# A gated mix of a Fourier layer and a feed-forward layer: sums of the hidden layer formed by adding stores, and the second Strassen level for more products

## The chip, the cores and the metric

One core of one Trainium2 chip. The metric is the device time of one execution in microseconds (us), the median of several runs. Engines by the profile's names: PE (TensorE, matmuls), PEld (its weight loads), DVE (VectorE), ACT (ScalarE), POOL (GpSimd) and SP (SyncE); the last two only issue DMAs here, ACT next to none.

## The reference, cut to what matters

```
g   = sigmoid((x * gate_w).sum(-1))                        # x: 2048 x 1024
a   = x @ dft_hid_re.T ;  b = x @ dft_hid_im.T             # 1024 x 1024 each
y   = dft_seq_re @ a - dft_seq_im @ b                      # 2048 x 2048 each
h   = relu(x @ w1 + b1) ** 2                               # w1: 1024 x 3584
o   = h @ w2 + b2                                          # w2: 3584 x 1024
out = g * y + (1 - g) * o
```

All in float32. The Fourier matrices are inputs like others; nothing of their structure is used.

## The kernel before, in words

**Five stages, one after the other on TensorE:** x (a and b from x), c (y, and y * g), h part 0 (hidden columns 0 to 2047), h part 1 (2048 to 3583), o (the output). What one stage gives the next goes through HBM in blocks of 128 partitions x 2 x 512 floats, 512 KB (class Kept: `ab`, `h_far`, `gy`).

**Float32 from three matmuls.** An operand block is split into `hi`, its value rounded to fp32r by a ScalarE copy, and `lo`, the remainder, by a VectorE subtraction (class Operand, lines 315 to 327). Each product of 128 x 128 by 128 x 512 is three matmuls: hi hi, hi lo, lo hi (Group.run, line 393). So each operand costs one ACT and one DVE instruction, and each sum of blocks one more of DVE.

**Seven products for eight.** Each stage is one 2 x 2 block product by the Strassen-Winograd scheme: sums S1 to S4 of left blocks, T1 to T4 of right blocks, seven products (FACTORS, line 49), worked in the order 1, 2, 5, 6, 3, 7, 4 (WIDE, TALL_C, TALL_O). Product 5 is S1 x T1, 6 is S2 x T2, 7 is S3 x T3, 4 takes T4; 1 and 2 take plain blocks. The results are added up on their way from PSUM by DVE (`add`) or copied by ACT (`put`); an ACT copy into PSUM (`prepare`, line 380) seeds a group with an earlier result.

**The second level.** `twice` works a product by the same scheme once more, on its own quarters, at the price of more sums, halves and takings-up. In the x and h stages ("wide", 2 x 2 k-steps) a product has the second level or not (TWICE_X, TWICE_H): 7 steps of 4 x 6 = 24 matmuls in place of 8 (of 18 in part 1). In c and o ("tall", 8 and 7 k-steps) TWICE_C and TWICE_O tell for each product how many pairs of k-steps have it; a pair is 84 matmuls then and 96 without. With FIRST_C, FIRST_O a product's remaining k-steps are worked ahead of the pairs, as groups of their own.

**Where sums are made.** Mostly by DVE, in the slot of the loaded block. LAND_X, LAND_C, LAND_H and LAND_O name sums of which some (the number is that of the stage's k-steps and halves) are made by POOL instead: SP loads the one block and an accumulating DMA of POOL's queue adds the other in SBUF (Part.load, lines 259 to 264). T2 (FAR_TALL) is formed from T1 as stored to HBM ("copy") and loaded again. S1 to S4 of x, made in the x stage, are kept in HBM for the h stages (`shared`).

**What sets the order.** Nothing is issued as written: every operation is recorded (class Op), and `plan` (line 1039) sorts them, by a model of times, into one order for each engine, with 55 slots of 4 KB per partition as SBUF (SLOTS), handed out by due time, and four PSUM pairs. A block's slot is free once its last reader is done, a store's landing included. `emit` (line 1181) issues them in that order, and that is why nearly all of the profile stands on line 1194. Each DMA queue has at most eight DMAs under way (LANES). POOL carries all stores and the accumulating DMAs, SP the plain loads.

**The h stages and o.** A result block of h belongs to F-half i and token-half n; `target` (line 822) names where it goes in HBM, `final` (line 832) applies bias, relu and square on ACT and puts one store on the list. In o the right operands are blocks `h_far[j, q, 2 * n + c]`, so T1 = h(0, 1) + h(0, 0) and T3 = h(1, 1) + h(0, 1) by F-half and token-half; T1 is made by accumulating loads (LAND_O) and T3 by DVE, 14 blocks each.

Of the kernel before, what the change touches and what calls it, by code (L numbers as in the profile page):

```python
# [15 lines left out]
P = 128  # L16
# [1 line left out]
NF = F // P  # L18
SLOTS = 55
WIDE, TALL_C, TALL_O = ((1, 2, 5, 6, 3, 7, 4),) * 3  # L20
TWICE_X, TWICE_C, TWICE_O = (1, 2, 5, 3, 4), {1: 1, 2: 4, 3: 4, 4: 4, 5: 2}, {1: 2, 2: 3, 3: 3, 4: 3, 5: 1}
FIRST_C, FIRST_O = (2,), (2,)
WARM = 44
FAR_TALL, FAR_WIDE = ("T2",), ()
LAND_X, LAND_C, LAND_H, LAND_O = {"T1": 4, "T3": 2}, {"T1": 16, "T3": 8}, ({"T1": 4}, {"T1": 2, "T3": 2}), {"T1": 14}
SHARE = ("S1", "S2", "S3", "S4")
TWICE_H = (1, 2, 5, 3, 4), (1, 2, 5, 3, 4)

MM, MM_END, FIRST_MM = 0.2267, 0.18, 6.2
VEC, VEC_END, ACT, ACT_END = (0.086, 1.0417e-3), 0.39, (0.11, 0.84e-3), 0.41  # L30
# [23 lines left out]
def gated_mix_kernel(ctx: ExitStack, tc: tile.TileContext, x4, xn, w4, ct, w1a, w1b, w2, b1, b2, gw, out):  # L54
# [168 lines left out]
    class Kept:  # L223


        def __init__(self, name):
            self.at, self.done, self.left = fixed([P, 2, 512], name, pool=dram), False, 2
            self.at.count, self.at.box = 1024, (0, 2, 0, 512)

        def store(self, src, k, tiles):  # L230

            nc.gpsimd.dma_start(self.at[:, k:k + tiles, :], src[:, :tiles, :])
            self.left -= tiles
            self.done = not self.left

# [178 lines left out]
    class Sums:  # L414


        def __init__(self, get, sums, keep=False, far=(), lands=(), shared=None):

            self.get, self.sums, self.keep, self.far, self.made = get, sums, keep, far, {}
            self.lands, self.shared = lands, shared  # L420

        def of(self, key, width=512, near=False):
            if key in self.made:
                return self.made[key]
            if self.shared and key in self.shared:
                return self.shared[key]
            if key not in self.sums:
                if not self.keep:
                    return self.get(*key)
                b = self.get(*key)  # L430
                e = b if isinstance(b, (Near, View)) else Part(b, width=width)
            else:
                a, b, op = self.sums[key]
                e = Part(*(self.of(p, width).far() if p in self.far and not near else self.of(p, width) for p in (a, b)),
                         op, width, key in self.lands)
                if self.shared is not None and key in SHARE:
                    self.shared[key] = e.far()
            self.made[key] = e
            return e
# [57 lines left out]
                    ends[e] = len(steps)  # L497
        return ends

    def tall(left, right, ksteps, order, second, first, target, final, last=None, lands={}):  # L500

# [7 lines left out]
        right = {(q, c): Sums(lambda j, n, q=q, c=c: right_(j, n, q, c), SUMS_R, far=FAR_TALL, lands=spread(lands, 2 * q + c, 2 * ksteps)) for right_ in (right,)  # L509
                 for q in range(ksteps) for c in range(2)}  # L510
        keys = [(c, rp) for c in range(2) for rp in range(2)]
        c11, c12, c21, c22 = ({k: target(i, n, k) for k in keys} for i in range(2) for n in range(2))
# [285 lines left out]
    def x_stage():  # L798
        to = {}

        def target(i, n, k):
            near = Near("ab")
            to[near] = ab[n, 4 * i + 2 * k[0] + k[2], k[1]]
            return near

        def final(dst, ps, sign):
            if ps is not None:
                nc.scalar.activation(flat(dst.slot), flat(ps), AF.Copy, scale=float(sign))
            stores.append((to[dst], dst, 0, 2))

        wide(lambda i, j, m, q: x4[2 * i + m, j, q], lambda j, n, q, c: w4[n, c, j, q], 4, WIDE, TWICE_X, target,
             final, -1, True, lands=LAND_X, shared=shared)

    h_far = {(j, q, t): Kept(f"h{j}{q}{t}") for j in range(2) for q in range(7) for t in range(4)}

    def h_stage(part):
        rows = 3 if part else 4
        to = {}  # L820

        def target(i, n, k):
            m, c, rp = k
            near = Near("h")
            tile0 = 16 * part + 2 * rows * i + rows * m + 2 * rp
            if rows == 4:
# [71 lines left out]
    def c_stage():  # L898
        rows = [Row(n, False) for n in range(2)]
        to = {}  # L900

        def target(i, n, k):
            near = Near("y")
            to[near] = i, n, *k
            return near

        def final(dst, ps):
            i, n, c, rp = to[dst]
            nc.vector.tensor_tensor(dst.slot, dst.slot if ps is None else ps, rows[n].of(c).broadcast_to([P, 2, 512]),
                                    op=ALU.mult)  # L910
            rows[n].used()
            stores.append((gy[i, n, c, rp], dst, 0, 2))

        at = len(steps)
        tall(lambda i, j, q: ab[j, q, i], lambda j, n, q, c: ct[n, c, j, q], 8, TALL_C, TWICE_C, FIRST_C, target, final,
             lands=LAND_C)
        return at, rows


    def o_stage():  # L920
# [25 lines left out]
        def final(dst, ps):  # L946
# [3 lines left out]
            for k in range(2):  # L950
# [285 lines left out]
```

## Time and profile before

| | |
|---|---|
| median of 3 runs | 1858.7 us (1857.58 to 1859.08) |
| the profiled execution | 1859.77 us, span 1858.0 us |
| PE busy | 1841.6 us, 8126 matmuls (44 of them to warm up) |
| DVE busy | 1706.1 us, 1692 instructions |
| ACT busy | 1096.3 us, 1254 instructions |
| POOL busy | 143.3 us |
| DMA | 445.06 MB, mean 240 GB/s |
| granted TensorE clock | 0.998 of full speed |

The span runs from the first to the last instruction; the execution's own time is a little longer. Every row of a view is one line of the kernel, engine, operation and tile; since one line emits everything, a row is known by its tiles: `lo<-raw,hi` is the subtraction that makes lo from a loaded block, `sum<-raw` a sum of two loaded blocks, `raw<-raw` one made in place, `both` a half-wide hi and lo in one slot, `u`, `ab`, `y`, `h`, `o` results on their way. "x1938 | 755.1, 390 | 7.5 <-ACT hi" is the number, the busy time in us, the mean ns of one, the engine's idle time ahead of them, and what ended most of it. Stretches of the span (windows) give each engine's busy time and number of instructions in it, the granted clock and the share of time in which the 16 DMA engines were busy.

### The profile page before, as it was taken

The page shows a single profiled execution, that of the slowest core. Times are in us where ns is not written, and L with a number is a line of the kernel's source. Part 1 is how long each engine was busy: PE and PEld are TensorE (multiplying, and loading weights), DVE is VectorE, ACT ScalarE, POOL GpSimd, SP SyncE. Part 2 cuts the span into 40 slices and gives each one's busy share as a digit, 9 for nine tenths or more (in the row PEclk, how much of TensorE's full clock was granted, in tenths as well). Part 3 has the DMA queues.
Part 4 walks back from the last instruction along what each step waited for, and adds up shares of the span by engine and source line. Part 5 has one row for each costly group of instructions (what it writes and reads, how often), then busy time and mean ns, then how long its engine had stood idle before and what let it go on. Part 6 is the DMA issues. An engine that isn't in the chain of part 4 may idle for free.

```text
span 1858.0 us, 22135 instructions
## 1 busy us (share of the span) xinstructions
PE 1841.6 (99%) x8126; PEld 1521.0 (82%) x8126; DVE 1706.1 (92%) x1692; ACT 1096.3 (59%) x1254; POOL 143.3 (8%) x230
## 2 busy tenths in 40 slices
PE   8999999999999999999999999999999999999998
PEld 7888887888888888888888888888788888888887
DVE  8997999799899997899995999968999988999998
ACT  6474656354453553466684799767986544355452
POOL 0100200001110001000100001001100111000001
PEclk9999999999999999999999999999999999999999
DMA  7762989449998479534661857537693899839835
GB/s 238 262 236 93 379 304 400 158 154 288 301 376 324 144 264 364 211 126 167 162 242 61 301 181 228 183 104 227 238 337 108 251 305 378 335 132 360 332 127 200
DMA packets 128862, 445.06 MB, mean 240 GB/s; under 512 B 14176, under 2 KB 23664, under 8 KB 128752
## 3 DMA queue, kind: packets, MB, share of 16 engines
q1 hardware_dynamic: 96544, 329.97, 48.5%
q0 software_dynamic: 31920, 113.27, 19.5%
q8 instruction: 64, 1.05, 0.2%
q10 hardware_dynamic: 288, 0.39, 0.1%
q14 instruction: 46, 0.38, 0.1%
HBM read 356.53 MB, written 87.04 MB: 239 GB/s over the span
## 4 chain that ended last, share of the span: by engine, by line
PE 86%; ACT 5%; DVE 4%; issue 3%; DMA 1%; POOL 0%; SPq 0%; DVEq 0%; POOLq 0%; ACTq 0%
PE ps L1194 86%; ACT h L1194 2%; ACT hi L1194 2%; DVE lo L1194 1%; DVE h L1194 1%; DVE sum L1194 1%; DMA raw<-in_ct 0%; DMA h<-h 0%; DMA raw<-in_x 0%; ACT u L1194 0%; ACT ps L1194 0%; POOL h L1194 0%; DVE o L1194 0%; DVE u L1194 0%; DVE raw L1194 0%
## 5 line engine op out<-in xcount | busy, mean ns | idle before, releaser
L1194 PE MATMUL ps<-hi 128*128 128x512 f32 x1938 | 755.1, 390 | 7.5 <-ACT hi L1194 4.7
L1194 PE MATMUL ps<-hi,lo 128*128 128x512 f32 x1938 | 753.7, 389 | 0.6 <-DVE lo L1194 0.6
L1194 PE MATMUL ps<-lo,hi 128*128 128x512 f32 x1938 | 753.9, 389 | 0.4 <-DVE lo L1194 0.4
L1194 ACT ACTIVATE hi<-raw 128x1024 fp32r<-128x1024 f32 (+2 forms) x375 | 380.4, 1034 | 250.2 <-DVE raw L1194 125.1
L1194 DVE TENSOR_TENSOR lo<-raw,hi 128x1024 fp32r<-128x1024 f32 (+2 forms) x375 | 441.1, 1194 | 44.1 <-ACT hi L1194 27.6
L1194 PE MATMUL ps<-hi,both 128*128 128x512 f32 x1512 | 467.0, 389 | 0.0
L1194 PEld LDWEIGHTS ps<-hi 128*128 128x128 f32 x1938 | 364.2, 188 | 86.7 <-ACT hi L1194 4.3
L1194 PEld LDWEIGHTS ps<-hi,lo 128*128 128x128 f32 x1938 | 364.0, 188 | 77.0 <-DVE lo L1194 1.0
L1194 PEld LDWEIGHTS ps<-lo,hi 128*128 128x128 f32 x1938 | 364.0, 188 | 76.3 <-DVE lo L1194 1.3
L1194 ACT ACTIVATE hi<-sum 128x1024 fp32r<-128x1024 f32 x228 | 233.3, 1035 | 190.8 <-DVE sum L1194 155.6
L1194 PEld LDWEIGHTS ps<-hi,both 128*128 128x128 f32 x1512 | 283.8, 188 | 59.3 <-ACT ps L1194 0.4
L1194 PE MATMUL ps<-lo,both 128*128 128x512 f32 x756 | 294.1, 389 | 0.0
L1194 DVE TENSOR_TENSOR lo<-sum,hi 128x1024 fp32r<-128x1024 f32 (+1 forms) x228 | 269.0, 1196 | 18.5 <-PE ps L1194 10.2
L1194 DVE TENSOR_TENSOR raw<-raw 128x1024 f32<-128x1024 f32 (+1 forms) x192 | 227.8, 1203 | 13.1 <-DMA raw<-h 3.6
L1194 DVE TENSOR_TENSOR sum<-raw 128x1024 f32<-128x1024 f32 (+2 forms) x168 | 171.8, 1031 | 6.0 <-PE ps L1194 3.0
L1194 ACT ACTIVATE u<-ps 128x1024 f32<-128x1024 f32 x110 | 106.4, 971 | 101.3 <-PE ps L1194 81.1
L1194 PEld LDWEIGHTS ps<-lo,both 128*128 128x128 f32 x756 | 141.9, 188 | 29.5
L1194 DVE TENSOR_TENSOR sum<-raw,sum 128x1024 f32<-128x1024 f32 (+2 forms) x126 | 137.8, 1095 | 4.7 <-PE ps L1194 3.6
L1194 DVE TENSOR_TENSOR h<-h,ps 128x1024 f32<-128x1024 f32 (+1 forms) x92 | 98.2, 1082 | 20.1 <-ACT u L1194 18.4
L1194 ACT ACTIVATE both<-sum 128x512 fp32r<-128x512 f32 x108 | 66.2, 624 | 54.6 <-DVE sum L1194 39.4
L1194 ACT ACTIVATE ps<-u 128x1024 f32<-128x1024 f32 x82 | 80.1, 978 | 24.7 <-DVE u L1194 6.9
L1194 ACT ACTIVATE h<-h,b1c 128x512 f32<-128x512 f32 x112 | 75.8, 709 | 4.3 <-DVE h L1194 4.1
(56 smaller groups left out, 814.3 us busy)
## 6 DMA issues: line engine op xcount, KB each, us to landing
raw<-in_ct SPq DMA_DIRECT2D x129, 512.0 KB, 7.9
raw<-h SPq DMA_DIRECT2D x120, 512.0 KB, 7.3
raw<-in_w SPq DMA_DIRECT2D x92, 512.0 KB, 8.3
raw<-ab SPq DMA_DIRECT2D x72, 512.0 KB, 9.3
raw<-copy SPq DMA_DIRECT2D x62, 512.0 KB, 4.9
raw<-in_x SPq DMA_DIRECT2D x59, 512.0 KB, 6.0
h<-h POOLq DMA_DIRECT2D x48, 512.0 KB, 4.4
copy<-raw POOLq DMA_DIRECT2D x46, 512.0 KB, 6.9
```

The source lines that it names most:

```text
L1194: made = getattr(real[op.engine], op.name)(*(actual(a) for a in op.args), **{k: actual(v) for k, v in op.kwargs.items()})
```

## The change

It makes T1 and T3 of h in HBM while h is written. For each k-step and half there is one more kept block for T1 and one for T3 (`sums_far`). A finished block of h is stored to each sum in which it has a part: the first store to a sum is plain, the second an accumulating one (Kept.store). The token-halves of o change places (`1 - n` in o's `target` and in its right operands), so that now T1 = h(0, 0) + h(0, 1) and T3 = h(0, 0) + h(1, 0) by F-half and token-half; h(0, 0), the first part of both, stands nowhere else and is no longer stored by itself. In o these sums are loaded as they are; T1 (NEAR_O) is loaded once into a slot and used from there.

The second level is given to product 6 of h part 0 (TWICE_H), to one more pair of k-steps of o's product 5 and to one pair of its product 6 (TWICE_O); product 2 of o no longer works its remaining k-step first (FIRST_O). POOL makes four T3 sums fewer in c, T1 and T3 four times each and not twice each in h part 1, and none in o (LAND_C, LAND_H, LAND_O).

```
-TWICE_X, TWICE_C, TWICE_O = (1, 2, 5, 3, 4), {1: 1, 2: 4, 3: 4, 4: 4, 5: 2}, {1: 2, 2: 3, 3: 3, 4: 3, 5: 1}
-FIRST_C, FIRST_O = (2,), (2,)
+TWICE_X, TWICE_C, TWICE_O = (1, 2, 5, 3, 4), {1: 1, 2: 4, 3: 4, 4: 4, 5: 2}, {1: 2, 2: 3, 3: 3, 4: 3, 5: 2, 6: 1}
+FIRST_C, FIRST_O = (2,), ()
...
-LAND_X, LAND_C, LAND_H, LAND_O = {"T1": 4, "T3": 2}, {"T1": 16, "T3": 8}, ({"T1": 4}, {"T1": 2, "T3": 2}), {"T1": 14}
+LAND_X, LAND_C, LAND_H, LAND_O = {"T1": 4, "T3": 2}, {"T1": 16, "T3": 4}, ({"T1": 4}, {"T1": 4, "T3": 4}), {}
 SHARE = ("S1", "S2", "S3", "S4")
-TWICE_H = (1, 2, 5, 3, 4), (1, 2, 5, 3, 4)
+NEAR_O = ("T1",)
+TWICE_H = (1, 2, 5, 3, 4, 6), (1, 2, 5, 3, 4)
...
     class Kept:
-        def __init__(self, name):
-            self.at, self.done, self.left = fixed([P, 2, 512], name, pool=dram), False, 2
+        def __init__(self, name, more=0):
+            self.at, self.done, self.left, self.more = fixed([P, 2, 512], name, pool=dram), False, 2 + more, more
...
         def store(self, src, k, tiles):
-            nc.gpsimd.dma_start(self.at[:, k:k + tiles, :], src[:, :tiles, :])
+            if self.left <= self.more:
+                nc.gpsimd.dma_start(self.at[:, k:k + tiles, :], src[:, :tiles, :], accum_op=ADD)
+            else:
+                nc.gpsimd.dma_start(self.at[:, k:k + tiles, :], src[:, :tiles, :])
...
     class Sums:
...
             if self.shared and key in self.shared:
-                return self.shared[key]
+                if key not in self.near:
+                    return self.shared[key]
+                self.made[key] = Part(self.shared[key])
+                return self.made[key]
...
-    h_far = {(j, q, t): Kept(f"h{j}{q}{t}") for j in range(2) for q in range(7) for t in range(4)}
+    h_far = {(j, q, t): Kept(f"h{j}{q}{t}") for j in range(2) for q in range(7) for t in range(4) if j + t // 2}
+    sums_far = {(q, c): {k: Kept(f"{k}{q}{c}", 2) for k in ("T1", "T3")} for q in range(7) for c in range(2)}
...
-            if rows == 4:
-                to[near] = h_far[i, 2 * m + rp, 2 * n + c], 0, 2, tile0
-            else:
-                to[near] = (h_far[i, 6, 2 * n + c], m, 1, tile0) if rp else (h_far[i, 4 + m, 2 * n + c], 0, 2, tile0)
+            q, at, tiles = (2 * m + rp, 0, 2) if rows == 4 else (6, m, 1) if rp else (4 + m, 0, 2)
+            far = [h_far[i, q, 2 * n + c]] if i + n else []
+            far += [sums_far[q, c][k] for k in (("T1", "T3"), ("T1",), ("T3",), ())[2 * i + n]]
+            to[near] = far, at, tiles, tile0
...
-            stores.append((kept, dst, at, tiles))
+            for k in kept:
+                stores.append((k, dst, at, tiles))
+            dst.uses = len(kept)
...
         def target(i, n, k):
             near = Near("o")
+            n = 1 - n
...
-        tall(lambda i, j, q: w2[i, j, q], lambda j, n, q, c: h_far[j, q, 2 * n + c], 7, TALL_O, TWICE_O, FIRST_O, target,
-             final, last, LAND_O)
+        tall(lambda i, j, q: w2[i, j, q], lambda j, n, q, c: h_far[j, q, 2 * (1 - n) + c], 7, TALL_O, TWICE_O, FIRST_O,
+             target, final, last, LAND_O, sums_far)
...
                 dst.store(src.slot, k, tiles)
-                src.used() if isinstance(src, Part) else src.drop()
+                src.used()
```

`tall` hands `shared` on to the sums of its right operands, and the other stages set `dst.uses = 1` for their single store.

More of the change, by code (lines that the diff above doesn't have):

```diff
@@ L414, in gated_mix_kernel, with __init__ @@
     class Sums:
-        def __init__(self, get, sums, keep=False, far=(), lands=(), shared=None):
+        def __init__(self, get, sums, keep=False, far=(), lands=(), shared=None, near=()):
+            self.near = near
             self.get, self.sums, self.keep, self.far, self.made = get, sums, keep, far, {}
@@ L498, in seven, with tall @@
         return ends
-    def tall(left, right, ksteps, order, second, first, target, final, last=None, lands={}):
+    def tall(left, right, ksteps, order, second, first, target, final, last=None, lands={}, shared=None):
         left = {q: Sums(lambda i, j, q=q: left_(i, j, q), SUMS_L, far=FAR_TALL) for left_ in (left,) for q in range(ksteps)}
-        right = {(q, c): Sums(lambda j, n, q=q, c=c: right_(j, n, q, c), SUMS_R, far=FAR_TALL, lands=spread(lands, 2 * q + c, 2 * ksteps)) for right_ in (right,)
+        right = {(q, c): Sums(lambda j, n, q=q, c=c: right_(j, n, q, c), SUMS_R, far=FAR_TALL, lands=spread(lands, 2 * q + c, 2 * ksteps),
+                               shared=shared and shared[q, c], near=NEAR_O) for right_ in (right,)
                  for q in range(ksteps) for c in range(2)}
@@ L809, in final @@
             stores.append((to[dst], dst, 0, 2))
+            dst.uses = 1
         wide(lambda i, j, m, q: x4[2 * i + m, j, q], lambda j, n, q, c: w4[n, c, j, q], 4, WIDE, TWICE_X, target,
              final, -1, True, lands=LAND_X, shared=shared)
-    h_far = {(j, q, t): Kept(f"h{j}{q}{t}") for j in range(2) for q in range(7) for t in range(4)}
+    h_far = {(j, q, t): Kept(f"h{j}{q}{t}") for j in range(2) for q in range(7) for t in range(4) if j + t // 2}
+    sums_far = {(q, c): {k: Kept(f"{k}{q}{c}", 2) for k in ("T1", "T3")} for q in range(7) for c in range(2)}
     def h_stage(part):
@@ L912, in final @@
             stores.append((gy[i, n, c, rp], dst, 0, 2))
+            dst.uses = 1
         at = len(steps)
```

## Prediction

> **What bounds the kernel now.** I read the page first, then its chain, then stretches of the span cut where one Strassen product ends and the next begins.
>
> ```profile
> span 1858.0 us, 22135 instructions
> PE 1841.6 (99%) x8126; PEld 1521.0 (82%) x8126; DVE 1706.1 (92%) x1692; ACT 1096.3 (59%) x1254; POOL 143.3 (8%) x230
> ...
> PE 86%; ACT 5%; DVE 4%; issue 3%; DMA 1%; POOL 0%; SPq 0%; DVEq 0%; POOLq 0%; ACTq 0%
> ...
> L1194 PE MATMUL ps<-hi 128*128 128x512 f32 x1938 | 755.1, 390 | 7.5 <-ACT hi L1194 4.7
> L1194 PE MATMUL ps<-hi,lo 128*128 128x512 f32 x1938 | 753.7, 389 | 0.6 <-DVE lo L1194 0.6
> L1194 PE MATMUL ps<-lo,hi 128*128 128x512 f32 x1938 | 753.9, 389 | 0.4 <-DVE lo L1194 0.4
> ...
> L1194 PEld LDWEIGHTS ps<-hi 128*128 128x128 f32 x1938 | 364.2, 188 | 86.7 <-ACT hi L1194 4.3
> ```
>
> The reader is to see that TensorE is busy all the time, and holds 86% of the chain; VectorE at 92% is close behind. Busy says nothing of pace: a row's 390 ns is the length of one pipelined matmul. The pace comes from a stretch without a stall, below: 520.0 us for 2295 matmuls is 0.2266 us each. The program has 8126 less 44 warm-up matmuls = 8082; at that pace they fill 1831.4 us. The other 26.6 us of the span are start, tail and stalls.
>
> ```profile
> core 0: us, PE busy (x) PEld busy (x) DVE busy (x) ACT busy (x) POOL busy (x), PEclk, DMA share, GB/s
> 49.20:125.30 76.10, 76.10 (x337) 63.02 (x336) 75.38 (x67) 42.85 (x44) 9.30 (x16) 1.00 0.71 242
> 320.00:840.00 520.00, 520.00 (x2295) 430.57 (x2295) 475.89 (x485) 256.36 (x297) 33.88 (x48) 1.00 0.71 247
> 695.40:782.50 87.10, 87.10 (x386) 72.12 (x385) 69.42 (x67) 37.07 (x41) 5.98 (x8) 1.00 0.84 298
> ...
> 896.70:972.90 76.20, 76.20 (x338) 63.10 (x337) 75.43 (x67) 58.48 (x65) 8.01 (x14) 1.00 0.63 209
> 972.90:1016.40 43.50, 43.50 (x194) 36.02 (x193) 22.82 (x20) 20.89 (x21) 0.70 (x2) 1.00 0.24 82
> 1016.40:1054.50 38.10, 38.10 (x170) 31.55 (x169) 37.40 (x34) 25.50 (x30) 2.14 (x4) 1.00 0.64 226
> 1054.50:1098.00 43.50, 43.50 (x194) 36.02 (x193) 39.17 (x35) 43.15 (x51) 4.27 (x8) 1.00 0.54 200
> 1098.00:1136.80 38.80, 38.67 (x170) 31.37 (x169) 38.80 (x37) 34.80 (x44) 4.82 (x9) 1.00 0.72 260
> 1136.80:1224.90 88.10, 86.55 (x379) 70.72 (x378) 84.45 (x88) 71.20 (x91) 8.24 (x13) 1.00 0.64 208
> ...
> 1319.10:1350.30 31.20, 29.16 (x128) 23.51 (x127) 30.61 (x34) 30.20 (x43) 4.87 (x10) 1.00 0.90 317
> 1350.30:1489.30 139.00, 138.99 (x613) 114.81 (x612) 133.25 (x146) 94.95 (x116) 9.30 (x13) 1.00 0.70 233
> 1489.30:1638.90 149.60, 149.60 (x661) 123.92 (x660) 132.65 (x125) 64.88 (x67) 16.60 (x25) 1.00 0.90 324
> 1638.90:1706.90 68.00, 68.00 (x301) 56.32 (x300) 67.11 (x72) 37.48 (x44) 0.00 (x0) 1.00 0.64 237
> 1706.90:1851.20 144.30, 144.30 (x637) 119.22 (x635) 141.56 (x147) 66.11 (x75) 7.19 (x10) 1.00 0.63 237
> ```
>
> Stalls can be read off: a stretch's length less its own matmuls (a row also counts the one or two across its edges) at 0.2266. 1098.0 to 1136.8 is product 4 of h part 0, 168 matmuls: 0.7 us lost. 1136.8 to 1224.9 is products 1, 2, 5 of part 1, 378 matmuls: 2.4 lost. 1319.1 to 1350.3 is product 4 of part 1, 126 matmuls: 2.6 lost. In all three DVE is busy almost without a break (38.80 of 38.80, 84.45 of 88.10, 30.61 of 31.20). So the bound is TensorE's count of matmuls, and where that bound is broken VectorE breaks it.
>
> **The Trainium skill** says otherwise on the first point. Its page "Perfetto Trace Analysis", section "Identifying the Most-Contended Engine", holds matmul occupancy to be no measure of the distance from the limit and puts the busy share of the weight loads in its place. By that, PEld at 82% would leave 18%, and a removed matmul would be worth a weight load at most: 48 of them, at the 188 ns of the LDWEIGHTS row, 9.0 us. Here the row of 320 to 840 differs: PEld is 83% where TensorE never waits, so 83% is the ceiling for this form, and I stay with the pace.
>
> **The change, part by part.** Counts are from the two programs' instruction lists.
>
> *Matmuls.* Product 6 of h part 0 takes the second level: 7 steps of 24 in place of 8, 24 fewer. In the output stage product 5 takes it for one more pair of k-steps and product 6 for a first pair; a pair is 84 matmuls in place of 96, so 24 fewer. Together 48, to 8034: 48 x 0.2266 = **10.9 us less**. Unsplitting product 2 (FIRST_O) changes no count.
>
> *VectorE.* The prices:
>
> ```profile
> L1194 DVE TENSOR_TENSOR lo<-raw,hi 128x1024 fp32r<-128x1024 f32 x347 | 417.2, 1219 | 37.6 <-ACT hi L1194 22.0 <-ACT u L1194 5.5 <-PE ps L1194 5.3
> L1194 DVE TENSOR_TENSOR both<-sum,both 128x512 fp32r<-128x512 f32 x108 | 72.9, 685 | 1.2 <-ACT both L1194 1.2
> L1194 DVE TENSOR_TENSOR raw<-raw 128x768 f32<-128x768 f32 x12 | 11.4, 953 | 2.7 <-DMA raw<-in_w1b 2.7
> ```
> ```profile
> 1103.04 1.22 DVE L1194 TENSOR_TENSOR h<-ps,u 128x1024 f32<-128x1024 f32 x1
> 1104.17 1.22 DVE L1194 TENSOR_TENSOR lo<-sum,hi 128x1024 fp32r<-128x1024 f32 x1
> 1105.30 1.22 DVE L1194 TENSOR_TENSOR h<-ps,u 128x1024 f32<-128x1024 f32 x1
> ```
>
> Back to back, one of 1024 starts 1.13 to 1.14 us after the one before, so 0.085 of its 1.22 overlaps; I take 1.135, and the same 0.085 off the others: 0.60 for 512, 0.87 for 768. Then:
> - h part 0, product 6: 6 more lo parts, 8 second-level sums, 14 more takings-up from PSUM (the adds onto c12 stay): 28 x 1.135 = +31.8 us.
> - Output stage: sums T1, T3 now arrive summed, so the 14 T3 adds go (T1's 14 were made by DMA already). Two more second-level pairs bring 2 lo, 14 half-wide lo, 8 sums, 8 half-wide sums, 8 takings-up: 4 x 1.135 + 22 x 0.60 = +17.8.
> - c stage: four T3 sums fewer are landed by DMA: +4.5. h part 1: four more are: -3.5.
>
> In all +50.6 us on an engine with 152 us idle. ScalarE's number of instructions does not change (1252); at 59% I cost it at nothing, covered by the matmuls.
>
> Whether it fits is a matter of place. I added up, for each stretch of matmuls, the VectorE work in its list up to the last instruction that these matmuls wait for, at the prices above (us; TensorE's time at 0.2266):
>
> | products | TensorE | VectorE due before | after |
> |---|---|---|---|
> | h part 0: 1, 2, 5 | 114.2 | 115.9 | 119.3 |
> | 6 | 43.5, after 38.1 | 20.4 | 37.5 |
> | 3 | 38.1 | 38.6 | 37.5 |
> | 7, 4 and h part 1: 1, 2, 5 | 167.2 | 162.4 | 167.0 |
> | h part 1: 6, 3 | 61.1 | 42.6 | 46.0 |
> | 7, 4 | 61.1 | 60.2 | 57.5 |
> | output: 1, 2 | 138.7 | 122.1 | 135.0 |
> | 5, 6 | 149.5, after 144.1 | 138.2 | 125.8 |
> | 3 | 68.0 | 59.3 | 80.0 |
> | 7, 4 | 144.1 | 135.2 | 135.0 |
>
> Product 6 of part 0 was VectorE's rest (22.82 of 43.50 busy); it now comes to 37.5 in 38.1. The trace shows that such products run without loss: 49.2 to 125.3 and 896.7 to 972.9 are pairs of them (75.4 of 76.1 and 75.43 of 76.20 busy, TensorE full). The 3.4 us more that are due in products 1, 2, 5, and as much in each of the two products ahead, can come from the rest in product 7 of c (69.42 of 87.10 busy). Then 167.0 us are due in 167.2 where 162.4 lost 3.1 (0.7 + 2.4) before: from nothing to the whole 4.6 more; I take +2, near the middle, as the margin falls from 4.8 to 0.2. Part 1's products 7, 4 have 2.7 less due: from -2.6 (that whole stall) to 0; I take -1. In the output stage product 3 is owed 12.0 more than its time, and products 5, 6 ahead of it have 18.3 spare: 0 if VectorE runs 12 us ahead, as c's product 7 shows it can (17.7 idle ahead of products with more due than their time), to 12.0 if it can't; I take +1, near the first. Stalls: **+2 us**.
>
> *Stores and loads.* 34 more DMAs on POOL's queue (260 for 226), 14 fewer on SP's (628 for 642). h's 64 stores become 48 (the h of F-half 0, token-half 0 is no longer kept by itself), and 64 stores of sums come, half of them adding. No store that adds into HBM is in the trace; nearest are the plain store and the adding load.
>
> ```profile
> q0 software_dynamic: 31920, 113.27, 19.5%
> ...
> h<-h POOLq DMA_DIRECT2D x48, 512.0 KB, 4.4
> ...
> raw<-h POOLq DMA_DIRECT2D x14, 512.0 KB, 10.0
> ```
> ```profile
> L1194 POOL DMA_DIRECT2D h<-h x64: 534/534/731, 921.8 to 1372.4; - x64
> ...
> L1194 POOL DMA_DIRECT2D raw<-h x14: 851/858/915, 1452.0 to 1525.4; - x14
> ```
>
> So one lies between 4.4 and 10.0 us to landing and between 0.53 and 0.86 us of POOL; I take 10 and 0.86, the row that adds. POOL's time is hidden behind an engine at 8%. The DMA engines have room: 0.24 to 0.72 busy over h part 0; 24 more stores of 512 KB there are 12.6 MB. POOL's queue (q0) moved 113.27 MB in 19.5% of 1858 us, 313 GB/s; so 40 us in 273, or 67 if the 16 that add move twice their bytes: 0.15 to 0.25 of share more. Each adding store waits on the store that it adds to; in POOL's list that stands at least 15 places earlier, and POOL lets only eight be under way, so this wait is over by the time POOL gets there. What is queued behind a waiting store are other stores, and the slot of h that both read comes free only with the second. That makes slots late, not matmuls, unless the free ones run out: 0 here, the rival below prices it. SP's queue gets shorter, and the output stage, its fullest (0.90 from 1489 to 1639), loses the 14 adding loads of T1 and 14 loads: from 0 to a little below.
>
> **Sum:** span 1858.0 - 10.9 + 2 = 1849.1. The profiled execution took 1859.77, 1.8 more than its span and 1.1 above the median of 1858.7; against the median, 1858.7 - 8.9 = **1849.8, so 1850**.
>
> **The rivals.**
> 1. *VectorE becomes the bound.* Against it: every row of the table but output 3 fits. For it: two rows have margins of 0.2 and 0.6 us in place of 4.8 and more, and no lost time is made up. Both upper ends paid, 4.6 + 12.0 = 16.6, gives 1858.7 - 10.9 + 16.6 = 1864; half of it 1856. I call it 1853.5 to 1862.
> 2. *The adding stores hold the slots: slower.* Place: the four bursts of h in which a finished half goes out (ends of products 3 and 4 in either part), eight tiles of two stores each, eight under way at a time. If a store lands at 10.0 in place of 4.4, the second round holds its slot 5.6 us longer, loads or operands have no slot, and TensorE waits: 4 x 5.6 = 22, 1858.7 - 8.9 + 22 = 1872. It decides for slower at 3.2 us a burst (8.9 + 3.7 over four). For it: the chain of before already runs through such a store, in the stretch that lost 2.6:
>
> ```profile
> 1328.94 7.46 DMA h<-h
> ```
>
> Against: 55 slots, and of those 2.6 us VectorE alone can be the cause. The Trainium skill ("DMA: Bandwidth & Descriptors", "Rules for kernel authors") says that an accumulate reads its destination and writes it later, with nothing holding the bytes between, so that it has to wait for the earlier DMA's semaphore. By that rule this wait is real; no run here shows it for HBM yet.
> 3. *Stalls shrink:* product 4 of part 1 loses nothing, nor does the output stage: 1858.7 - 10.9 - 2.6 = 1845.
> That the change doesn't do what it says is out: the lists show 48 matmuls fewer and the 32 adding stores.
>
> **How the numbers follow.** Forecast, 1846 to 1853.5: 0.62. Rival 1: 0.20. Rival 2: 0.08. Rival 3, 1846 and below: 0.10. A measurement of this kernel can tell about 0.2%, 3.7 us, from no change. Faster than 1855.0: 0.62, 0.10 and 0.08 of rival 1 make 0.80; within, the rest of rival 1: 0.12; slower: 0.08. The range: 1845 to 1857.5, which leaves out rival 2, the top of rival 1 and a little of rival 3.
>
> **What would show it.** Right: 8078 matmuls, 0.2266 apart outside the stalls; product 6 of part 0 near 38 us with VectorE full; VectorE's busy time near 1750; stalls beside start and tail near 10 us. Wrong: TensorE waiting on lo or sum over output product 3 (rival 1), on POOL's stores or landings near the ends of the h parts (rival 2); adding stores landing much later than 10 us.

## The result, and the profile after

The changed kernel takes **1852.6 us** (median; 1851.9 to 1854.4), the one before 1858.7 beside it: a ratio of 0.9969, 95% interval 0.9958 to 0.998. The forecast was 1850.0 in a range of 1845.0 to 1857.5. The profiled execution took 1852.40 us with a span of 1850.6; the one of before 1859.77 and 1858.0. Between the two spans lie 7.4 us, between the two medians 6.1.

The page of the kernel after: busy time and chain, then the two large DMA queues, then the stores (512 KB each, median us to landing).

```profile
span 1850.6 us, 22073 instructions
PE 1831.6 (99%) x8078; PEld 1511.9 (82%) x8078; DVE 1753.4 (95%) x1746; ACT 1090.8 (59%) x1254; POOL 169.2 (9%) x264
...
q1 hardware_dynamic: 94016, 323.15, 48.0%
q0 software_dynamic: 37072, 127.43, 22.5%
...
PE 82%; DVE 7%; ACT 4%; issue 3%; DMA 3%; POOL 0%; SPq 0%; DVEq 0%; ACTq 0%; POOLq 0%
...
T<-h POOLq DMA_DIRECT2D x48, 512.0 KB, 10.0
```

The 48 matmuls are gone (8126 to 8078), VectorE has its 47 us more (1706.1 to 1753.4), and TensorE's part of the chain falls from 86 to 82%, for VectorE 7 (4), DMA 3 (1). Where that sits is seen in stretches cut at the products' ends, as in the prediction: h part 0 products 6, 7, 4; part 1 products 1, 2, 5 together, and 4; output products 5 and 6 together, and 3.

```profile
973.30:1011.40 38.10, 38.10 (x170) 31.52 (x169) 37.77 (x35) 11.39 (x12) 0.00 (x0) 1.00 0.38 125
1049.40:1093.00 43.60, 43.60 (x194) 36.08 (x193) 39.97 (x35) 41.18 (x49) 10.81 (x16) 1.00 1.04 331
1093.00:1134.30 41.30, 38.57 (x169) 31.34 (x168) 40.80 (x38) 37.45 (x48) 8.44 (x13) 1.00 0.74 247
1134.30:1221.90 87.60, 86.63 (x380) 70.76 (x380) 87.21 (x90) 73.13 (x94) 19.30 (x29) 1.00 0.95 299
1316.00:1346.50 30.50, 29.13 (x127) 23.50 (x126) 30.34 (x34) 28.54 (x41) 9.54 (x15) 1.00 0.96 313
1485.50:1629.70 144.20, 144.20 (x638) 119.38 (x637) 143.44 (x145) 77.15 (x86) 10.46 (x18) 1.00 0.73 259
1629.70:1699.10 69.40, 68.30 (x301) 56.22 (x300) 68.57 (x74) 43.91 (x51) 0.00 (x0) 1.00 0.61 214
```

In the order of the columns: length; busy time and number on PE, PEld, DVE, ACT, POOL; clock; DMA share; GB/s. A stretch's own matmuls at 0.2265 us, taken from its length before rounding, leave what it lost (us; the prediction took 0.2266, which moves none of the first four differences):

| stretch | before | after | difference | forecast |
|---|---|---|---|---|
| h part 0, product 4 | 0.75 | 3.33 | +2.6 | +2 for this row and the next |
| h part 1, products 1, 2, 5 | 2.54 | 1.89 | -0.6 | (in the row above) |
| h part 1, product 4 | 2.65 | 1.97 | -0.7 | -1 |
| output product 3 | 0.05 | 1.49 | +1.4 | +1 |
| start of the x stage, tail | 11.43 | 12.28 | +0.8 | 0 |
| all else | 3.56 | 3.54 | 0.0 | 0 |

48 x 0.2265 = 10.9 less and 3.5 more lost make the 7.4 of the spans. The sizes are near the forecast; what doesn't fit is that product 4 of part 0, which the forecast held no worse than its neighbours, now loses as much by itself as the first two rows together did before. Here are the longest wait of TensorE between 1030 and 1350 us (total, times, longest), then the chain of the same place, in order of time (start, length, what), and then ScalarE's wait for one of the loads issued from 1045 to 1092 us.

```profile
PE ps L1209 <- DVE h L1209: 2.3, 1, 2.3
```
```profile
1029.87 36.05 PE ps L1209 x159
...
1065.94 16.02 DMA raw<-in_x
...
1081.99 1.06 ACT hi L1209
1083.06 1.23 ACT h L1209 x2
```
```profile
  ACT hi L1209: 2.1, 1
```

TensorE waits for VectorE; but the chain goes on back, from VectorE (nearly without a break from 1094 to 1140 us) to ScalarE and from there to one load of x that took 16.0 us to land, in the stretch whose DMA share is 1.04 (it was 0.54; the share of a stretch can come out a little over 1). Of before, that stretch's row in the prediction also tells what the forecast didn't read from it: ScalarE was busy 43.15 of 43.50 us there already.

**The theories.** *DMA:* the adding stores fill the DMA engines over product 7 of part 0, a load is late, and behind it everything is. *VectorE:* it has more due than there is time for, as the forecast had it, and the late load only happens to be there. A third came up on the way: *ScalarE* has no rest in that product and hands the lateness on.

### The profile page after: what moved, and what is told of

Read it like the earlier page. It is cut to its first block, busy times and chain, and to the rows that moved or that the text cites. A ratio compares the mean times of both kernels' runs of the same rounds, so it can differ in the third digit from the quotient of the medians.

```text
span 1850.6 us, 22073 instructions
## 1 busy us (share of the span) xinstructions
PE 1831.6 (99%) x8078; PEld 1511.9 (82%) x8078; DVE 1753.4 (95%) x1746; ACT 1090.8 (59%) x1254; POOL 169.2 (9%) x264
## 3 DMA queue, kind: packets, MB, share of 16 engines
q0 software_dynamic: 37072, 127.43, 22.5%
## 4 chain that ended last, share of the span: by engine, by line
PE 82%; DVE 7%; ACT 4%; issue 3%; DMA 3%; POOL 0%; SPq 0%; DVEq 0%; ACTq 0%; POOLq 0%
PE ps L1209 82%; DVE lo L1209 3%; ACT h L1209 2%; DMA raw<-in_x 2%; ACT hi L1209 2%; DVE h L1209 1%; DVE o L1209 1%; DVE sum L1209 1%; DMA raw<-in_ct 0%; DMA h<-h 0%; DVE u L1209 0%; DVE both L1209 0%; ACT ps L1209 0%; DVE raw L1209 0%; POOL h L1209 0%
## 5 line engine op out<-in xcount | busy, mean ns | idle before, releaser
L1209 PE MATMUL ps<-hi 128*128 128x512 f32 x1866 | 727.0, 390 | 8.6 <-ACT hi L1209 3.5
L1209 PE MATMUL ps<-hi,lo 128*128 128x512 f32 x1866 | 725.9, 389 | 0.6 <-DVE lo L1209 0.6
L1209 PE MATMUL ps<-lo,hi 128*128 128x512 f32 x1866 | 725.7, 389 | 0.4 <-DVE lo L1209 0.4
L1209 PE MATMUL ps<-hi,both 128*128 128x512 f32 x1624 | 501.9, 389 | 1.1 <-DVE both L1209 1.1
L1209 ACT ACTIVATE hi<-sum 128x1024 fp32r<-128x1024 f32 x244 | 249.7, 1036 | 198.3 <-DVE sum L1209 140.2
L1209 PEld LDWEIGHTS ps<-hi,both 128*128 128x128 f32 x1624 | 304.7, 188 | 65.2 <-DVE both L1209 1.9
L1209 PE MATMUL ps<-lo,both 128*128 128x512 f32 x812 | 315.9, 389 | 0.0
L1209 DVE TENSOR_TENSOR lo<-sum,hi 128x1024 fp32r<-128x1024 f32 (+1 forms) x244 | 288.2, 1196 | 12.3 <-PE ps L1209 8.8
L1209 DVE TENSOR_TENSOR raw<-raw 128x1024 f32<-128x1024 f32 (+1 forms) x178 | 211.1, 1205 | 5.6 <-DMA raw<-in_x 1.8
L1209 DVE TENSOR_TENSOR sum<-raw,sum 128x1024 f32<-128x1024 f32 (+2 forms) x135 | 147.5, 1094 | 3.7 <-PE ps L1209 2.8
L1209 ACT ACTIVATE both<-raw 128x512 fp32r<-128x512 f32 x87 | 53.8, 624 | 46.3 <-DVE raw L1209 21.2
```

Source lines behind the costliest of these rows:

```text
L1209: made = getattr(real[op.engine], op.name)(*(actual(a) for a in op.args), **{k: actual(v) for k, v in op.kwargs.items()})
```

## The experiments

**1. All adding stores issued as plain ones, in the same order.**

```
+        keep = {k: v for k, v in op.kwargs.items()
+                if k != "accum_op" or getattr(op.args[0].base, "name", "")[:1] != "T"}
```

> The changed kernel, every instruction in the same place, but the 32 adding stores of T1 and T3 are issued as plain stores (the second overwrites the first, so T1 and T3 hold one term only). Theory A, VectorE: product 4 of h part 0 loses 3.3 us because VectorE has more due than it has time; then nothing changes there, 3.3 us lost, time 1852.6. Theory B, DMA: the adding stores fill the DMA engines from 1040 to 1090 us, a load of x lands after 16 us and the operands behind it are late; then the loss falls to about 0.8 us as before the change, and the time is near 1850. Output product 3 loses 1.5 us by both.

1849.9 us, 0.9953 (0.9937 to 0.997). Every T1 and T3 of h holds one of its two terms alone. Product 4 of part 0 lost 1.10; part 1's products 1, 2, 5 lost 1.9 and output product 3 lost 1.48, both as in the changed kernel. The two stretches of products 7 and 4 of part 0, and the queue of POOL's DMAs, in this run:

```profile
1049.30:1092.80 43.50, 43.50 (x194) 36.03 (x193) 41.45 (x37) 43.19 (x51) 8.52 (x16) 1.00 0.83 337
1092.80:1131.90 39.10, 38.31 (x169) 31.45 (x168) 39.06 (x37) 35.25 (x46) 6.92 (x13) 1.00 0.71 259
```
```profile
q0 software_dynamic: 36560, 127.43, 20.4%
```

The same bytes on POOL's queue take 20.4% of 1848.3 us in place of 22.5% of 1850.6: 377 and 416 us of all 16 engines. So adding costs 39 us over 14.7 MB (24 stores of 512 KB, 8 of 256), about 1.4 us for each 512 KB, where 512 KB of this queue cost 1.6 on the mean (377 us for 127.43 MB, its accumulating loads included). An adding store is about two plain ones. VectorE has the same work, and the 2.2 us at product 4 are gone: the theory DMA holds there. Output product 3 loses the same with and without adding.

**2. VectorE relieved, in the same order.** Eight in-place adds of h and four of o work on half their columns.

```
+HALF = {("h", "ps"): range(28, 36), ("o", "u"): range(1, 4), ("o", "ps"): range(5, 6)}
...
+            if seen[kind] in HALF.get(kind, ()):
+                args = [a[:, 0:1, :] if len(a.shape) == 3 else a[:, 0:512] for a in args]
```

> The changed kernel, every instruction in the same place, but twelve in-place adds of VectorE work on half of their columns (the other half keeps the earlier value): eight of h between 1082 and 1125 us, 8 x 0.53 = 4.3 us less work, and four of o between 1646 and 1656 us, 2.1 us less. Theory A, VectorE: product 4 of h part 0 loses at most 1 us in place of 3.3, and output product 3 nothing in place of 1.5: 1849. Theory B, DMA: product 4 of part 0 still loses 2 to 3.3 us, output product 3 nothing: 1851.

1850.4 us, 0.9958 (0.9943 to 0.9972). The halves left out are missing from h and o. Product 4 of part 0 lost 0.14 although the load still took 15.4 us; but part 1's product 1 lost 2.48 in place of 0.99, and output product 3 lost 0.40. So both are right for product 4: the load comes late, and VectorE has nothing to make it up with. Part of the gain is lost again 40 us on, behind a second late load (11.1 us of the chain). That load is as late in the changed kernel (11.4 us from issue to landing, 6.0 in the kernel before); there, behind the loss at product 4, products 1 and 2 of part 1 lost only 1.3. Output product 3 follows VectorE's work.

**3. Without the second level of product 6 of part 0**, planned anew.

```
-TWICE_H = (1, 2, 5, 3, 4, 6), (1, 2, 5, 3, 4)
+TWICE_H = (1, 2, 5, 3, 4), (1, 2, 5, 3, 4)
```

> The changed kernel without the second level for product 6 of h part 0, planned anew: 24 matmuls more, 5.4 us. Theory A, VectorE: with its rest in product 6 back, product 4 of part 0 loses 0.8 us as before the change: 1852.6 + 5.4 - 2.5 = 1855.5. Theory B, DMA: the stores are still there, product 4 still loses about 3 us: 1858.

1862.9 us, 1.0025 (1.0014 to 1.0036): slower than before the change. Both numbers missed. The profiled execution was the slowest of the seven, 1866.8 us, so the losses that follow are above those of the median. VectorE has its rest in product 6 back (24.4 us idle), and yet product 4 of part 0 lost 5.0 us and part 1's product 1 lost 6.8. The two long DMAs of this run's chain between 1000 and 1200 us, its waits of TensorE from 1000 to 1360, and three stretches:

```profile
1055.03 23.16 DMA raw<-in_w1a
1143.52 17.20 DMA raw<-in_x
```
```profile
PE ps L1209 <- DVE u L1209: 3.9, 1, 3.9
PE ps L1209 <- DVE h L1209: 3.7, 3, 2.9
```
```profile
1130.00:1134.00 4.00, 1.10 (x5) 0.56 (x4) 4.00 (x5) 4.00 (x6) 1.12 (x3) 1.00 1.02 159
1134.00:1142.00 8.00, 7.96 (x28) 6.43 (x29) 7.12 (x7) 7.94 (x12) 5.81 (x9) 0.79 1.06 318
1164.00:1176.00 12.00, 8.12 (x25) 6.22 (x24) 11.41 (x12) 7.41 (x10) 5.95 (x6) 0.72 1.09 322
```

Loads land after 17 and 23 us, TensorE stands for 2.9 and 3.9 us, and behind each stall the granted clock is half for a while ((1 - 0.79) x 8 x 2 = 3.4 us and, from 0.72 over 12 us, 6.7). With less for VectorE to do it got worse, so VectorE's work alone doesn't set the loss. Since the plan is another one, the run doesn't part the stores from the place that the plan gives the loads.

**4. The output stage's second level as before**, the sums still made by adding stores; planned anew.

```
-TWICE_X, TWICE_C, TWICE_O = (1, 2, 5, 3, 4), {1: 1, 2: 4, 3: 4, 4: 4, 5: 2}, {1: 2, 2: 3, 3: 3, 4: 3, 5: 2, 6: 1}
-FIRST_C, FIRST_O = (2,), ()
+TWICE_X, TWICE_C, TWICE_O = (1, 2, 5, 3, 4), {1: 1, 2: 4, 3: 4, 4: 4, 5: 2}, {1: 2, 2: 3, 3: 3, 4: 3, 5: 1}
+FIRST_C, FIRST_O = (2,), (2,)
```

> The changed kernel with the output stage's second level as before (product 5 one pair, product 6 none, product 2's last k-step first), planned anew; sums by adding stores stay. 24 matmuls more, 5.4 us; VectorE has 13.2 + 20.4 = 33.6 us less to do there, so output product 3 loses nothing, 1.5 us less: 1856.5. If instead the stall of product 3 came from loads, it would stay: 1858.

1858.1 us, 0.9999 (0.999 to 1.0009). VectorE's busy time is 31.0 us less than in the changed kernel (1722.4 for 1753.4), and output product 3 lost 0.05, as expected if that work causes the stall. The profiled executions are 6.2 us apart, of which the 24 matmuls are 5.4. The rest nearly cancels: 1.4 less in output product 3, 0.8 more in product 4 of part 0, 2.2 more in part 1's, and 0.8 less in all else. The clock fell to half once:

```profile
1124.96:1128.37 3.41, 1.19 (x6) 0.72 (x5) 3.38 (x5) 3.38 (x6) 2.32 (x4) 1.00 1.04 303
1128.37:1131.78 3.41, 3.41 (x9) 2.64 (x9) 3.41 (x4) 3.38 (x6) 0.71 (x2) 0.50 1.05 317
1340.00:1343.41 3.41, 2.13 (x10) 1.43 (x8) 3.41 (x5) 3.38 (x7) 1.44 (x2) 1.00 0.92 299
1343.41:1346.83 3.42, 1.53 (x7) 1.31 (x8) 3.42 (x6) 3.42 (x6) 1.45 (x2) 1.00 1.03 222
1346.83:1350.24 3.41, 3.41 (x17) 2.80 (x16) 3.41 (x4) 3.38 (x6) 1.35 (x3) 1.00 1.07 207
```

Nine matmuls in 3.4 us against seventeen, those across the edges counted: the first stall (2.2 us) cost the clock, the longer one from 1341 on (3.2 us) didn't. The last section tells why.

**5. Four accumulating loads fewer in part 1**, that is two T1 and two T3 as before the change; planned anew.

```
-LAND_X, LAND_C, LAND_H, LAND_O = {"T1": 4, "T3": 2}, {"T1": 16, "T3": 4}, ({"T1": 4}, {"T1": 4, "T3": 4}), {}
+LAND_X, LAND_C, LAND_H, LAND_O = {"T1": 4, "T3": 2}, {"T1": 16, "T3": 4}, ({"T1": 4}, {"T1": 2, "T3": 2}), {}
```

> The changed kernel with part 1 of h landing two T1 and two T3 sums by DMA instead of four and four, as before the change: four accumulating loads of w1b fewer around the end of part 0, their adds (3.5 us) back on VectorE. Theory DMA: what the crowd costs at product 4 of part 0 (3.3 us) shrinks to 1.1 to 2.5, the rest of the h stage as it was: 1850.5 to 1852. Theory VectorE (that stretch has no margin, every us due there is lost): +3.5 us, about 1856.

1863.4 us, 1.0025 (1.0014 to 1.0035). Both numbers missed again. Product 4 of part 0 lost 3.9 (no better), and part 1's product 4 lost 8.5 and output product 1 lost 4.5. It looks the same one part on, ahead of and in part 1's product 4 (a row of the chain, one of TensorE's waits, two stretches):

```profile
1287.67 23.19 DMA raw<-in_x
```
```profile
PE ps L1209 <- ACT u L1209: 4.9, 2, 4.5
```
```profile
1318.00:1330.00 12.00, 7.54 (x26) 5.74 (x27) 11.37 (x12) 11.97 (x18) 1.08 (x2) 0.81 0.76 267
1330.00:1340.00 10.00, 10.00 (x41) 8.16 (x40) 7.79 (x9) 8.52 (x12) 3.70 (x7) 0.89 0.79 288
```

A load took 23.2 us while the stores of product 3 of part 1 went out, ScalarE stood behind it, TensorE waited 4.5 us for ScalarE, and the clock was at half for 6.8 us (2 x (0.19 x 12 + 0.11 x 10)). Over product 7 of part 0 the DMA share was 1.04 here too, so those four accumulating loads are not what fills the DMA engines there; and the 3.5 us of VectorE's work don't account for the 10.8 us that the run is slower than the changed kernel's first median. The late loads stand in the burst of stores behind product 3 of either part. Plain stores were not tried in this plan.

**6. Another order: the planner's LATE at 40 instead of 80.**

> The changed kernel with one number of its planner changed (how late an operation may be put, 80 to 40): same instructions, another order on VectorE, ScalarE and SP. Theory DMA and theory VectorE agree on 1850 to 1855: it tells how much of the 5.2 us lost in products 7, 4 of part 0 and 1, 2, 5 of part 1 hangs on the order alone. If that stretch loses under 3.5 us, the time is near 1850.5 and the loss is one of placing; if it loses 5 us or more in another place, the work due there is what counts.

1851.8 us, 0.9962 (0.9948 to 0.9977). Product 4 of part 0 lost 3.5 and products 1, 2, 5 of part 1 lost 1.9, as in the changed kernel; output product 3 lost 0.07. Order alone heals the output stage, where VectorE only has to be ahead in time, and not the h stage.

**7. Without the second level of output product 6** (one pair, 12 matmuls more).

```
-TWICE_X, TWICE_C, TWICE_O = (1, 2, 5, 3, 4), {1: 1, 2: 4, 3: 4, 4: 4, 5: 2}, {1: 2, 2: 3, 3: 3, 4: 3, 5: 2, 6: 1}
+TWICE_X, TWICE_C, TWICE_O = (1, 2, 5, 3, 4), {1: 1, 2: 4, 3: 4, 4: 4, 5: 2}, {1: 2, 2: 3, 3: 3, 4: 3, 5: 2}
```

> The changed kernel without the pair of k-steps of output product 6 on the second level: 12 matmuls more (2.7 us), some 9 us of VectorE less in the output stage. If the 1.5 us lost in output product 3 comes from VectorE being owed more than that product's time, it goes: 1852.6 + 2.7 - 1.4 = 1853.9, product 3 losing under 0.3 us. If something else makes it (loads), product 3 still loses 1.5: 1855.3. The h stage is planned as in the changed kernel and loses what it did.

1854.6 us, 0.9979 (0.9969 to 0.9989). Output product 3:

```profile
1632.10:1700.10 68.00, 68.00 (x301) 56.31 (x300) 66.96 (x72) 43.85 (x51) 0.00 (x0) 1.00 0.62 219
```

68.00 us, nothing lost, as VectorE's theory had it (its busy time fell by 20.4 us in all, to 1733.0, more than the 9 expected). The pair is worth 2.7 us and gave 1.4 back there.

**8. Product 6 of part 0 alone, on the kernel before** (no adding store, output stage as before).

```
-TWICE_H = (1, 2, 5, 3, 4), (1, 2, 5, 3, 4)
+TWICE_H = (1, 2, 5, 3, 4, 6), (1, 2, 5, 3, 4)
```

> The kernel before with only one part of the change: product 6 of h part 0 takes the second level (24 matmuls fewer, 5.4 us, 31.8 us of VectorE more); h is stored as before, no store adds, and the output stage is as before. Start: 1858.7 - 5.4 = 1853.3. Theory VectorE (the rest in product 6 is what was lost, and the wait at product 4 of part 0 comes from that): products 7, 4 of part 0 and 1, 2, 5 of part 1 lose 2 us more than the 3.3 us of before, 1855.3, with product 4 of part 0 over 2.5 us by itself. Theory DMA (the stores of sums crowd out the loads at the end of part 0, and without them no load is late): they lose 3.3 to 4 us as before, DMA share over product 7 under 0.8, 1853.3 to 1854.

1856.7 us, 0.9989 (0.998 to 0.9998): 5.4 us of matmuls gone, 2.3 won. That is above what either theory expected. Products 7, 4 and part 1's 1, 2, 5 lost 5.4 in place of 3.3, and product 3 of part 0, where neither theory put a loss, 1.7; product 4 itself only 1.4. No load is in its chain there. The chain from 1035 to 1110 us and the stretches of products 3 and 7:

```profile
by line: ACT h L1194 39.2%; ACT hi L1194 25.1%; issue 11.9%; ACT u L1194 10.3%; ACT ps L1194 7.7%; DVE lo L1194 3.0%; DVE h L1194 1.6%; DVE sum L1194 1.5%; ACTq L1194 0.1%
```
```profile
1010.00:1049.70 39.70, 38.88 (x169) 31.14 (x167) 39.39 (x36) 20.48 (x24) 1.60 (x3) 1.00 0.42 143
1049.70:1094.60 44.90, 44.26 (x193) 36.01 (x194) 43.09 (x39) 44.58 (x53) 4.26 (x8) 1.00 0.64 237
```

82% of it is ScalarE, which is busy 44.58 of 44.90 us. So the loss of VectorE's rest can cost some 3.8 us without any adding store; but in run 1, with the same work of VectorE in part 0 in the changed kernel's order, these products lost 3.1 in all. What makes the one order bear it and the other not was not settled. What it gave is the third theory: ScalarE in product 7.

**9. Only the eight adding stores over product 7 of part 0 plain**, the changed kernel's order.

```
+        if "accum_op" in keep and getattr(op.args[0].base, "name", "")[:1] == "T":
+            adding += 1
+            if adding <= 8:
+                del keep["accum_op"]
```

> The changed kernel in its own order, with only the first 8 adding stores (those issued from 1040 to 1073 us, over product 7 of part 0) issued as plain ones, so that these 8 blocks of T sums hold one summand alone; the other 24 add. Theory DMA, narrowed to this place: the extra traffic of these 8 is the part of the 32 that makes the load of x late, so product 4 of part 0 loses 1.1 us as with all 32 plain (3.3 now), the rest as in the changed kernel: 1850.4. Rival: all 32 adding stores matter by their sum, or what the run with all 32 plain won came from somewhere else; then product 4 of part 0 still loses 2.5 to 3.3, 1852 to 1852.6.

1851.8 us, 0.9963 (0.995 to 0.9975), beside 1852.5 of the changed kernel (run 12). Products 7 and 4:

```profile
1049.70:1093.20 43.50, 43.50 (x194) 36.02 (x193) 41.46 (x37) 43.18 (x51) 8.49 (x16) 1.00 0.84 336
1093.20:1132.30 39.10, 38.32 (x169) 31.45 (x168) 39.06 (x37) 35.26 (x46) 8.46 (x13) 1.00 0.72 228
```

Product 4 lost 1.06, as with all 32 plain. From 1040 to 1092 us the issues of the two kernels read, first the changed one's, then this one's:

```profile
h<-h POOLq DMA_DIRECT2D x11, 512.0 KB, 13.5
T<-h POOLq DMA_DIRECT2D x8, 512.0 KB, 17.5
...
raw<-in_x SPq DMA_DIRECT2D x5, 512.0 KB, 14.4
```
```profile
h<-h POOLq DMA_DIRECT2D x11, 512.0 KB, 6.4
T<-h POOLq DMA_DIRECT2D x8, 512.0 KB, 9.2
...
raw<-in_x SPq DMA_DIRECT2D x5, 512.0 KB, 8.7
```

Eight stores that add make the transfers around them take 1.7 to 2.1 times as long (1.6 for the loads of w1a). The queue of POOL's DMAs takes 21.9% of 1851.1 us, 11 us of all 16 engines less than in the changed kernel, again 1.4 for each store made plain. The expected time (1850.4) was missed, and the 0.7 us to the changed kernel lie within the spread of the executions: products 1 and 2 of part 1 now lost 3.4 in place of 1.3 to 1.7, behind the second crowd, which still adds. The load of x in the chain there took 14.2 us to land, 8.2 with all stores plain (run 1).

**10. ScalarE relieved right behind the late load**, the changed kernel's order.

```
+HALF = {"relu": range(34, 40), "square": range(17, 19)}
...
+            if seen[kind] in HALF[kind]:
+                args[:2] = [a[:, 0:256] if len(a.shape) == 2 else a[:, 0:1, :] for a in args[:2]]
```

> The changed kernel in its own order, all 32 stores adding; six Relu and two Square of h on ScalarE, those from 1083.0 to 1092.4 us right behind the late load of x, work on half their columns (the other half of these blocks stays without them): 6 x 0.21 + 2 x 0.43 = 2.1 us, as much as ScalarE stood waiting for that load. Theory ScalarE has no margin there (43.2 of 43.5 us busy in this product before the change, and only VectorE's work that hangs on it comes late): product 4 of part 0 loses 1.1 to 1.4 us in place of 3.3 to 3.6, 1850.3 to 1850.6. Theory VectorE alone (it has no margin, ScalarE's lateness costs it little): product 4 still loses 2.5 or more, 1852 or above.

1851.4 us, 0.9962 (0.9949 to 0.9976). The halves left out go without Relu or Square. The load took 15.6 us again, the DMA share was 1.04 again, and product 4 lost 0.94:

```profile
1049.50:1093.10 43.60, 43.60 (x194) 36.08 (x193) 41.70 (x37) 41.59 (x52) 10.81 (x16) 1.00 1.04 332
1093.10:1132.00 38.90, 38.27 (x169) 31.40 (x168) 38.87 (x37) 34.77 (x45) 8.44 (x13) 1.00 0.76 247
```

2.1 us given back to ScalarE brought TensorE 2.4 to 2.7: ScalarE hands the lateness on. As in run 9 the second crowd took part of it (products 1 and 2 of part 1 lost 3.2).

**11 and 12. LATE at 40 again, and the changed kernel again, side by side.**

> The changed kernel with the planner's LATE at 40 again, in more rounds and beside the changed kernel on the same chip: 1.4 us less lost in output product 3, as its first profile shows, so 1.2 to 1.6 us below the changed kernel, unless its medians differ by less than their spread (0.5 us), in which case the order is no improvement that can be measured.

> The changed kernel unaltered, beside the three others on the same chip: 1852.6 as before, 0.9969 of the kernel before.

1850.6 us (1850.6 to 1852.0), 0.9958 (0.9944 to 0.9971), against 1852.5 (1851.6 to 1853.7), 0.9966 (0.9953 to 0.9978). Output product 3 lost 0.05 against 1.50. It is the fastest version here that leaves nothing out, 0.8 us below the changed kernel's first median in run 6 and 1.9 us below it side by side, though the intervals of the ratios overlap.

## Why the prediction was right

**The matmuls:** right. Product 6 of part 0 went from 43.5 to 38.1 us, 0.225 for each of the 24 that left. Had weight loads been the measure, as the prediction took it from the Trainium skill ("Perfetto Trace Analysis", "Identifying the Most-Contended Engine"), it would have been at most 24 of them at 188 ns, 4.5 us; the 5.4 measured decide for the pace.

**VectorE's work:** right in size (+47.3 of busy time for +50.6 of starts).

**Stalls, +2:** +3.5, of which 0.8 are the start and the tail, which no run tells a cause of. Product 4 of part 1 (-0.7 for -1) and output product 3 (+1.4 for +1) came as reckoned, and runs 2, 4 and 7 show that the second is VectorE's, owed more than its time; no run was made for the first. VectorE did run ahead as the forecast hoped (143.44 of 144.20 busy over products 5 and 6), not quite far enough; runs 6 and 11 show that the order decides the rest.

**The first +2 had the right size and, in the main, the wrong reason, so its size is luck.** It was put to VectorE's margin of 0.2 us in 167.2. Runs 1, 9 and 10 show the cause at product 4 of part 0, whose +2.6 is more than all of the +1.9: eight adding stores, a load of x landing after 16 us instead of 9, ScalarE waiting 2.1 us for it, and neither ScalarE nor VectorE able to make it up. Run 2 shows that VectorE's want of margin belongs to it, as its last link. But a stall that is healed there comes back in part in the next burst: over products 7, 4 and part 1's 1, 2, 5 together run 9 lost 5.1 and run 10 lost 4.7, where the changed kernel lost 5.3 and 5.9 (its two profiles) and the kernel before 3.3. Only with all the stores plain (run 1) did that sum come to 3.0. So in this order all the adding stores, not those eight alone, are behind the +1.9. The steps that failed are two, and both took a mean for a place:
- "The DMA engines have room": 0.15 to 0.25 of share more was spread over all of part 0. The mean of the part rose by only 0.09, from 0.57 to 0.66 (below), but the stores go out in one burst, and product 7 went from 0.54 to 1.04.
- "At 59% I cost it at nothing": ScalarE in product 7 was at 43.15 of 43.50 us in a row that the prediction itself shows.

```profile
858.60:1136.80 278.20, 278.07 (x1226) 229.60 (x1225) 251.33 (x222) 210.55 (x237) 22.48 (x40) 1.00 0.57 194
```
```profile
859.00:1134.30 275.30, 272.57 (x1201) 225.04 (x1200) 269.75 (x238) 194.17 (x221) 35.20 (x55) 1.00 0.66 214
```

**Rival 2** named the right place (the burst behind product 3) and resource, and the wrong carrier: not slots held by stores, since the late load was issued on time, at 1065.94 in the changed kernel and 1065.78 in run 1, when a matmul freed its slot, and only took longer (16.0 and 9.2 us). Its price of 22 us was paid nowhere. Two orders of the whole change were run and both won (runs 11 and 12); but two close variants, planned anew, came out slower than before by 0.25%, with loads of 17 to 23 us and stalls that halve the clock (runs 3 and 5). That their adding stores make those loads late is likely and not shown, since neither was run with plain stores. How near to a loss the change lies, the chances (0.08 for slower) did not see.

**The adding store:** 10.0 us to landing and 0.86 us of POOL were assumed for the store itself. In the page all T stores of 512 KB land in 10.0 (7.3 when none adds), and over product 7 those that add in 17.5, with 0.91 us of POOL for each (0.53 when plain, run 1). Its wait, which the Trainium skill ("DMA: Bandwidth & Descriptors", "Rules for kernel authors") calls for, cost nothing that shows: over the whole kernel POOL stood 2.1 us, once, for a store of T.

## What to carry to other kernels

Cost DMAs that leave in a burst against the stretch in which they leave, not against the stage, and an adding store into HBM as about two plain ones. Read every engine's row in that stretch: ScalarE, idle for 41% of the whole span and full right there, passed a late load on in full. A stall healed in one place can come back at the next one, so judge a cure by the sum of a stage. And where a planner sets the order, the result has a spread of its own (two orders of this change gave -0.3% and -0.4%, two close variants +0.25%): a gain of this size belongs to its order.

## What was not expected of the hardware

An accumulating store into HBM took about 1.4 us of all 16 DMA engines for 512 KB on top of the 1.6 of this queue's mean without them (run 1, and the same from run 9's eight); no row of the trace of before shows that price.

Stalls of TensorE cost more than their length, but not always: the granted clock was at half for 3.4 us behind a stall of 2.2 us (run 4), one of 2.9 (run 3) and one of 2.0 (run 5), for twice that behind 3.9 and 4.5 (runs 3 and 5), and not at all behind 2.3 (the changed kernel) and 3.2 (run 4). The Trainium skill ("TensorE: Matmul & The Clock Gate", "Part 1: The HAM clock gate (the 'warmup' mystery)") has the clock fall after an idle window of about 3.4 us and rise after as long a busy one. Half clock for once or twice 3.4 us agrees with that length; a fall behind 2.0 us of waiting does not follow from it.

What decides can be read from the traces. Within a run, the changes of the granted clock lie whole multiples of 3.413 us apart: 1134.35, 1137.77, 1168.49 and 1175.31 in run 3 (1, 10 and 12 of them from the first), 1325.42, 1332.25, 1407.34 and 1410.76 in run 5 (2, 24 and 25). Between two such places lies a window; counted on from the half clock of the warm-up, which begins at 11.72 us, the changed kernel has an edge at 1127.88. First two windows of the changed kernel, then two of run 5:

```profile
1124.47:1127.88 3.41, 2.00 (x9) 1.31 (x7) 3.38 (x5) 3.38 (x5) 1.43 (x2) 1.00 0.98 312
1127.88:1131.30 3.42, 2.53 (x11) 2.12 (x12) 3.42 (x4) 3.39 (x6) 1.44 (x2) 1.00 1.04 307
```
```profile
1403.93:1407.34 3.41, 1.38 (x6) 0.86 (x5) 3.41 (x4) 3.41 (x5) 0.00 (x0) 1.00 0.64 199
1407.34:1410.75 3.41, 3.41 (x9) 2.63 (x9) 3.41 (x5) 1.39 (x3) 0.00 (x0) 0.50 0.91 339
```

The changed kernel's stall lies across an edge, 1.41 us of idle time on one side and 0.89 on the other, as does the second one of run 4 (1.28 and 1.89, in its rows above); run 5's of 2.03 lies in one window. From 20 to 1840 us, in all fourteen traces, half clock followed each window at full clock in which TensorE stood for 2.03 us or more (2.94 and 2.65 in run 3, 2.22 in run 4, 3.10 and 2.03 in run 5) and none in which it stood for 1.89 or less. Since the edges fall elsewhere in each execution, a stall of 2 to 3.7 us may by this cost 3.4 us of half clock or nothing. The ten executions of run 4 took from 1856.5 us, at a mean granted clock of 1.000, to 1862.5, at 0.995.
